# Three first loads on two queues: ScalarE's pair waits for a write of zeros, and two row blocks change queues

## The chip, the cores and the metric

The kernel runs on one core of a Trainium2 chip. The metric is the device time of one execution in microseconds (us). Before the change three runs took 220.27, 220.36 and 220.91 us, so the median is 220.36 us.

A core has five engines that run their own instruction lists and wait for each other by semaphores: TensorE (PE in the profile, its weight loads PEld), VectorE (DVE), ScalarE (ACT), GpSimd (POOL) and SyncE (SP). SP, ACT and POOL can also issue DMA transfers; all transfers are carried by the core's 16 DMA engines.

## What is computed

The input x has 2048 rows of 512 elements (bf16). Rows are normalised (mean and variance, no learned scale), and the result is the sum of x itself and of two branches over the normalised rows:

```python
xn = _layernorm(x)
# branch A: 32 heads of 16; features are softmax(+) and softmax(-) of q @ w_phi and k @ w_phi
kv  = einsum("bhsf,bhsd->bhfd", phi_k, v);  z = sum over s of phi_k
o   = (phi_q @ kv) / (phi_q @ z + 1e-6)
A   = o @ wo
# branch B: a gated product without a nonlinearity
B   = ((xn @ w_gate) * (xn @ w_up)) @ w_down        # 512 -> 1792 -> 512
out = x + A + B
```

q, k and v come from one matrix wqkv (512 x 1536); only its last third, wv, plays a part near the change.

## The kernel before, in words

The 2048 rows are cut into 16 blocks of 128 rows, x0 to x15, which lie in one tile `xall` (128 partitions x 16 blocks x 512). Four blocks make a group. Weights stay in SBUF: `wv` (the v third of wqkv, four chunks of 128 rows), `wg` and `wu` (gate and up), `wd` (down), `wo`, `wphi`, and `wT2`, which holds the k and q thirds of wqkv transposed.

The order on each engine is the order of the program text; nothing is rearranged by a scheduler. A tracker adds the semaphore waits that reads after writes, and writes after writes, need.

**The loads at the start** (lines 82 to 103). SP's queue issues x0, x2 and the second half of wv (chunks 2 and 3), then pieces of wg and wu, wphi, the transposed k third (wT2), x4 to x7, more of wg and wu, x8 to x15, wd and wo. ScalarE first loads its table and runs a one-column activation (`first`, line 90), and its queue issues x1 and the first half of wv (chunks 0 and 1). GpSimd's queue issues x3. Before its first real work VectorE fills small constants: `mhalf` (line 108) and the ones columns of five `vt` tiles (line 136).

**Warm-up.** TensorE has nothing to do until x arrives, so `warm_up` (line 309) gives it nine matmuls on a constant, seven of 512 columns and two of 128.

**The first four blocks** (lines 371 to 406). For a short way from the load to the first matmul these blocks are treated apart from the rest: instead of a full normalisation, `sub_sum` (line 338) writes D*x minus the row sum, and the row's scale is applied later.

- The row sums: block 0 by VectorE (`sum_of`, line 374), blocks 1 and 2 by ScalarE (line 378, an activation that also accumulates; the trace shows it as an ACTIVATE and a READ_ACCUMULATOR), block 3 by VectorE.
- `sub_sum` for all four on VectorE, block 0 in two halves.
- `lt` (line 206): four 128x128 transposes on TensorE per block, into one PSUM bank, and copies (line 207) into `xnT` by VectorE or ScalarE.
- `first_v` (line 237): x @ wv for a block, in two steps of two chunks; chunks 0 and 1 need the first half of wv, chunks 2 and 3 the second. The tiles are called kv for blocks 0 and 1 and pv for blocks 2 and 3.

VectorE's list at this place is: sum of x0, `sub_sum` of x0 (two halves), `sub_sum` of x1 (needs ScalarE's sum), two copies of block 0's transposes, `sub_sum` of x2, a copy of block 1, sum of x3, and so on. TensorE's list is: transposes of block 0, of block 1, `first_v(0)` chunks 0 and 1, transposes of block 2, `first_v(1)` and `first_v(2)` chunks 0 and 1, `first_v(0)` chunks 2 and 3, transposes of block 3, the rest of `first_v`, and then the long sequence of gate and up matmuls (`ffn`, lines 275 and 279), k and q features, attention and output (`fin`, lines 291 and 294), which fills the remaining time.

Of the kernel before, what the change touches and what calls it, by code (L numbers as in the profile page):

```python
# [21 lines left out]
def kernel(  # L22
# [12 lines left out]
    nc = tc.nc  # L35
    P = 128
    S, D = A_x.shape[-2], A_x.shape[-1]
# [19 lines left out]
    xall = xpool.tile([P, NT, D], BF16)  # L57
# [10 lines left out]
    def dma_x(lo, hi, eng=nc.sync):  # L68
        eng.dma_start(out=xall[:, lo:hi, :], in_=x_view[:, lo:hi, :])
# [4 lines left out]
    def dma_wv(lo, hi, eng):  # L74
        eng.dma_start(out=wv[:, lo:hi, :],
                      in_=A_wqkv[lo * P:hi * P, 2 * D:3 * D].rearrange("(c p) f -> p c f", p=P))
# [3 lines left out]
        dma_cols(nc.sync, wu, B_w_up, lo, hi)  # L80

    dma_x(0, 1)
    dma_x(2, 3)
    dma_wv(2, DC, nc.sync)

    ET = mybir.EngineType
# [1 line left out]
    ones = nc.const_aps.tensor(1.0, [P, P], BF16)  # L88
    first = consts.tile([P, 1], BF16)
    nc.scalar.activation(out=first[:], in_=ones[:, 0:1], func=AF.Exp, scale=1.0)  # L90
    dma_x(1, 2, nc.scalar)
    dma_wv(0, 2, nc.scalar)
    dma_x(3, 4, nc.gpsimd)
    dma_gu(0, 2 * P)
# [431 lines left out]
```

## Time and profile before

| | |
|---|---|
| median of three runs | 220.36 us |
| the profiled execution's own time | 220.46 us |
| its span (first to last instruction) | 218.8 us |
| TensorE matmul busy | 214.9 us, 98% of the span |
| VectorE, ScalarE, GpSimd busy | 64%, 41%, 34% of the span |
| granted TensorE clock | 1.00 in every stretch |
| TensorE's first warm-up matmul starts | 0.83 us |
| its first transpose starts | 4.34 us |
| its first matmul with wv starts | 5.20 us |

How to read it: the profile page has shares of busy time, a chain of work that ended last, and groups of instructions by line. The timeline lists instructions with their start and duration, both in us from the span's start; "x8" means eight instructions merged into one row, "[0.41 <-DVE xn L338]" that the engine had been idle for 0.41 us and what released it. A name such as ACTq or SPq is an engine's sequencer, which issues the DMAs. In the list of DMA issues the last number is the time from issue to landing. In the table of DMA queues q1 is SP's, q10 ScalarE's and q0 GpSimd's; the columns are packets, MB and the share of the 16 engines' time in the window asked for. A packet of x or of wv is one row of 512 bf16 elements, so a block of x is 128 packets. Matmuls are pipelined, so a TensorE row's duration overlaps the next one's, and the pace is read from start to start.

### The profile page before, as it was taken

Reading aid. Unit: us, or ns where it says so; the run is one execution under the profiler, and the core shown is the slowest. Engines: PE = TensorE matmul, PEld = TensorE weight load, DVE = VectorE, ACT = ScalarE, POOL = GpSimd, SP = SyncE. Lnnn points to the kernel's source line nnn. Section 1 sums busy time; section 2 is a strip of 40 time slices with the busy share of each in tenths; the row PEclk is TensorE's granted clock in tenths of the full one; section 3 lists DMA queues with packets and bytes.
Section 4 is the critical chain, followed back from the end, with each engine's and each line's share of the span. In section 5 each row is a group of like instructions: output and inputs, shape, how many; then the busy total and the mean of one; then the engine's idle time right before and its main releaser. Section 6 shows DMA issues by size and latency. Waiting matters only on the chain.

```text
span 218.8 us, 3493 instructions
## 1 busy us (share of the span) xinstructions
PE 214.9 (98%) x1291; PEld 103.1 (47%) x1291; DVE 141.0 (64%) x242; ACT 89.2 (41%) x159; POOL 74.9 (34%) x72
## 2 busy tenths in 40 slices
PE   8999999999999999999999999999999999999994
PEld 3444445454444444444544444444444444454443
DVE  4878867786598758576599773296655655454321
ACT  5545686569575875565435212141231322100000
POOL 4450843373357554636045333033123033000000
PEclk9999999999999999999999999999999999999999
DMA  5999996005202240202028355114461431412201
GB/s 198 286 297 372 372 219 136 2 0 51 48 0 49 51 94 2 48 3 48 1 43 105 76 114 114 37 24 96 96 70 30 95 72 28 96 48 72 69 30 48
DMA packets 48433, 19.91 MB, mean 91 GB/s; under 512 B 37504, under 2 KB 48384, under 8 KB 48416
## 3 DMA queue, kind: packets, MB, share of 16 engines
q1 hardware_dynamic: 47952, 19.16, 38.9%
q10 hardware_dynamic: 416, 0.39, 0.5%
q8 instruction: 10, 0.16, 0.3%
q0 software_dynamic: 48, 0.13, 0.2%
q14 instruction: 7, 0.06, 0.1%
HBM read 8.67 MB, written 2.10 MB: 49 GB/s over the span
## 4 chain that ended last, share of the span: by engine, by line
PE 97%; DMA 1%; DVE 1%; issue 0%
PE g L275 22%; PE fin L291 22%; PE u L279 22%; PE fin L294 6%; PE q L237 6%; PE k L237 6%; PE pv L237 6%; PE kv L331 2%; PE ab L465 2%; DMA xall<-in_A_x_dram 1%; PE kv L237 1%; PE tp L206 1%; PE pq L226 1%; DVE tot L374 0%; DVE xn L338 0%; DVE o_sb L301 0%
## 5 line engine op out<-in xcount | busy, mean ns | idle before, releaser
L275 PE MATMUL g<-xnT,wg 128*128 128x512 bf16 x224 | 57.5, 379 | 0.0
L279 PE MATMUL u<-xnT,wu 128*128 128x512 bf16 x224 | 57.5, 379 | 0.0
L254 POOL TENSOR_TENSOR phiq<-e,rsum 128x1024 bf16<-128x1024 f32 x16 | 30.9, 1933 | 63.5 <-DVE rsum L252 56.0
L283 DVE TENSOR_TENSOR hT<-u,g_sb 128x512 bf16<-128x512 f32 x56 | 37.0, 666 | 23.9 <-PE u L279 15.8
L282 ACT CAST g_sb<-g 128x512 bf16<-128x512 f32 x56 | 32.9, 587 | 46.8 <-PE g L275 46.5
L250 DVE TENSOR_REDUCE sums<-e 128x64 f32<-128x1024 f32 x32 | 38.9, 1216 | 20.1 <-ACT e L247 20.1
L291 PE MATMUL fin<-wd,hT 128*128 128x512 bf16 (+2 forms) x238 | 51.1, 366 | 0.0
L254 POOL TENSOR_TENSOR phik<-e,rsum 128x1024 bf16<-128x1024 f32 x16 | 30.9, 1932 | 39.6 <-DVE rsum L252 33.6
L279 PEld LDWEIGHTS <-wu 128*128 128x128 bf16 x224 | 21.9, 98 | 26.4
L291 PEld LDWEIGHTS <-hT 128*128 128x128 bf16 x238 | 22.4, 98 | 24.8
L275 PEld LDWEIGHTS <-wg 128*128 128x128 bf16 x224 | 21.1, 98 | 24.0
L237 PEld LDWEIGHTS <-xnT 128*128 128x128 bf16 x192 | 17.4, 98 | 18.2 <-ACT xnT L207 0.7
L301 DVE TENSOR_TENSOR o_sb<-fin,xall 128x512 bf16<-128x512 f32 (+2 forms) x13 | 8.5, 651 | 20.5 <-PE fin L294 20.5
L252 DVE RECIPROCAL rsum<-sums 128x64 f32<-128x64 f32 x32 | 17.7, 553 | 3.1
L294 PE MATMUL fin<-wo,oT 128*128 128x512 bf16 (+2 forms) x68 | 16.6, 366 | 0.0
L237 PE MATMUL k<-W1k,xnT 128*128 128x512 bf16 x64 | 16.4, 379 | 0.0
L237 PE MATMUL q<-W1q,xnT 128*128 128x512 bf16 x64 | 16.4, 378 | 0.0
L246 ACT ACTIVATE e<-q 128x512 f32<-128x512 f32 x12 | 7.2, 597 | 22.2 <-PE q L237 22.2
L237 PE MATMUL pv<-wv,xnT 128*128 128x512 bf16 x56 | 14.4, 379 | 0.0
L478 DVE TENSOR_TENSOR otok<-ab,rden 128x512 bf16<-128x512 f32 x16 | 11.1, 692 | 0.6
L323 ACT CAST vt<-pv 128x512 bf16<-128x512 f32 x12 | 7.0, 587 | 10.0 <-PE pv L237 10.0
L154 DVE BATCH_NORM_STATS2 stats<-xall 128x6 f32<-128x512 bf16 x16 | 10.6, 664 | 0.0
(63 smaller groups left out, 131.8 us busy)
## 6 DMA issues: line engine op xcount, KB each, us to landing
out_dram<-o_sb SPq DMA_DIRECT2D x15, 128.0 KB, 2.0
wd<-in_B_w_down_dram SPq DMA_DIRECT2D x1, 1792.0 KB, 15.8
xall<-in_A_x_dram SPq DMA_DIRECT2D x1, 1024.0 KB, 11.9
wg<-in_B_w_gate_dram SPq DMA_DIRECT2D x1, 640.0 KB, 7.7
wu<-in_B_w_up_dram SPq DMA_DIRECT2D x1, 640.0 KB, 10.4
xall<-in_A_x_dram SPq DMA_DIRECT2D x1, 512.0 KB, 4.5
wg<-in_B_w_gate_dram SPq DMA_DIRECT2D x1, 512.0 KB, 5.3
wu<-in_B_w_up_dram SPq DMA_DIRECT2D x1, 512.0 KB, 6.4
```

The source lines that it names most:

```text
L154: nc.vector.bn_stats(out=stats[:], in_=xall[:, n, :])
L237: nc.tensor.matmul(ps, lhsT=xnT[:, j, n * P:(n + 1) * P], rhs=w[:, j, :], start=(j == 0), stop=(j == DC - 1))
L250: nc.vector.tensor_reduce(out=sums[:], in_=ev, axis=AX.X, op=ALU.add)
L252: nc.vector.reciprocal(out=rsum[:].rearrange("p a b -> p (a b)"), in_=sums[:])
L254: nc.gpsimd.tensor_tensor(out=phi[:].rearrange("p g (x f) -> p (g x) f", f=DH), in0=ev, in1=rsum[:].to_broadcast((P, 2 * H, DH)), op=ALU.mult)
L275: nc.tensor.matmul(gps, lhsT=wg[:, c, f * P:(f + 1) * P], rhs=xnT[:, c, T * TT:(T + 1) * TT], start=(c == 0), stop=(c == DC - 1))
L279: nc.tensor.matmul(ups, lhsT=wu[:, c, f * P:(f + 1) * P], rhs=xnT[:, c, T * TT:(T + 1) * TT], start=(c == 0), stop=(c == DC - 1))
L282: nc.scalar.copy(out=g_sb[:], in_=gps)
L283: nc.vector.tensor_tensor(out=hTs[T][:, f, :], in0=ups, in1=g_sb[:], op=ALU.mult)
L291: nc.tensor.matmul(ps, lhsT=hTs[T][:, f, t4 * P:(t4 + 1) * P], rhs=wd[:, f, lo:lo + w], start=(f == 0), stop=False)
L294: nc.tensor.matmul(ps, lhsT=oTs[n][:, c, :], rhs=wo[:, c, lo:lo + w], start=False, stop=(c == DC - 1))
L478: nc.vector.tensor_tensor(out=o_tok[:].rearrange("p (b h d) -> p b h d", b=2, d=DH), in0=abv[:, :, :, 0:DH], in1=rden[:].to_broadcast((P, ...
```

## The change

SP's second load becomes x1 instead of x2, and ScalarE's first load becomes x2 instead of x1. In front of ScalarE's loads VectorE gets one new instruction, at the head of its list: it writes zeros over the first 256 columns of block 2 in `xall`. ScalarE's load of x2 writes the same bytes, so it must wait for that write, and the load of wv's first half stands behind it in the same list. The values are all overwritten by the load. In the built program the write is a memset of 128 words per partition, ScalarE's first load waits for a VectorE semaphore, and no other instruction of any engine is added or removed; ScalarE's first row sum (x1) now waits for SP's second load, its second (x2) for its own queue's first.

```diff
     dma_x(0, 1)
-    dma_x(2, 3)
+    dma_x(1, 2)
     dma_wv(2, DC, nc.sync)
...
     nc.scalar.activation(out=first[:], in_=ones[:, 0:1], func=AF.Exp, scale=1.0)
-    dma_x(1, 2, nc.scalar)
+    nc.vector.memset(xall[:, 2, 0:D // 2], 0.0)
+    dma_x(2, 3, nc.scalar)
     dma_wv(0, 2, nc.scalar)
     dma_x(3, 4, nc.gpsimd)
```

## The prediction

> **What bounds the kernel now.** I read the chain of work that ended last first, on the page and then in order of time for the first 16 us.
>
> ```profile
> PE 97%; DMA 1%; DVE 1%; issue 0%
> ```
>
> ```profile
> 0.79 2.45 DMA xall<-in_A_x_dram
> ...
> 3.27 0.70 DVE tot L374
> ...
> 3.99 0.30 DVE xn L338
> ...
> 4.34 1.07 PE tp L206 x8
> 5.40 0.54 PE kv L237 x2
> ...
> 9.50 0.86 PE g L275 x4
> ```
>
> From 4.34 us on the chain is TensorE to the end, and the table of stretches has TensorE busy in every us from 5.20 to 214. So a delay before TensorE's first wv matmul is passed on to the end, and a gain there is all that this change can bring; what I have to find is when that matmul (5.20) starts afterwards. The timeline of the first 8 us and the finer rows of VectorE and TensorE show what it waits for:
>
> ```profile
> 0.79 1.28 ACT L90 ACT_TABLE_LOAD   x1 [0.79 <-PEq L510]
> ...
> 0.85 0.40 ACTq L69 DMA_DIRECT2D xall<-in_A_x_dram  x1
> 0.86 0.06 DVE L108 MEMSET mhalf<- 128x4 f32 x1 [0.86 <-PEq L510]
> 1.00 0.62 DVE L136 MEMSET vt<- 128x32 bf16 x5
> ...
> 1.28 0.45 ACTq L75 DMA_DIRECT2D wv<-in_A_wqkv_dram  x1
> ...
> 3.57 0.63 ACT L378 ACTIVATE junk<-xall 128x512 bf16<-128x512 bf16 x1 [1.28 <-DMA xall<-in_A_x_dram]
> ...
> 4.11 0.19 ACT L378 ACTIVATION_READ_ACCUMULATOR junk<-xall 128x1 f32 x1
> ```
>
> ```profile
> 4.39 0.35 DVE L338 TENSOR_SCALAR xn<-xall,tot 128x512 bf16<-128x512 bf16 x1
> ```
>
> ```profile
> 4.77 0.29 DVE L207 COPY xnT<-tp 128x256 bf16<-128x256 bf16 x1
> ```
>
> ```profile
> 4.80 0.39 PE L206 MATMUL tp<-ident,xn 128*128 128x128 bf16 x2
> ```
>
> x1 lands at 0.85 + 2.7 = 3.55, ScalarE starts its sum at 3.57 and has it at 4.11 + 0.19 = 4.30, VectorE subtracts it at 4.39, TensorE transposes block 1 from 4.80. VectorE's list is in order, so the copy of block 0's transposes (4.77) also stands behind the subtraction for x1, although block 0 had been ready before. Block 0's way (x0 lands at 3.25, its sum, its two halves at 3.99 and 4.19) ends on VectorE at the same 4.39. x1's landing therefore has only about 0.05 us of slack: sum at 4.30, a handover of 0.05 (VectorE's first half ends at 4.28, TensorE's weight load starts at 4.33), subtraction at 4.39.
>
> **The change, part by part.**
>
> *The write of zeros.* A memset of 4 words takes 0.06 and one of 32 elements 0.09, so about 1.07 ns an element; 128 words give 0.06 + 124 x 1.07 ns = 0.19 us. Bounds: 0.09 (the 32-element row) and 0.33 (all 256 elements one by one). It starts where mhalf does, 0.86, and ends at 1.05. VectorE's other memsets move from their end at 1.62 to about 1.85; its next work is at 3.27, so this costs nothing.
>
> *ScalarE's wait.* With the handover of 0.05 its first load is issued at 1.10 instead of 0.85, 0.25 late (0.15 to 0.39), and wv's first half at 1.53 instead of 1.28. Behind the waiting instruction stand only that load and the sums of x1 and x2, which need x anyway. wv's first half lands at 1.53 + 3.4 = 4.93 (4.68 before), and TensorE wants it at 5.20 or later: covered by 0.27, and by more once TensorE is late itself. If that cover goes, see the second rival. x2 lands at 1.10 + 2.7 = 3.80, up to 4.0; its sum starts only behind that of x1, at 4.33 before: covered.
>
> *x1 in second place of SP's queue.* This is the price of the change. In the list of DMA issues ScalarE's first load (x1) and SP's second (x2) show the same 2.7 us to landing:
>
> ```profile
> xall<-in_A_x_dram ACTq DMA_DIRECT2D x1, 128.0 KB, 2.7
> xall<-in_A_x_dram SPq DMA_DIRECT2D x1, 128.0 KB, 2.7
> ```
>
> SP's second load is issued at 1.25, so x1 lands at 3.95 if nothing else changes: the upper bound, 0.40 later. The lower bound comes from the packets of the queues (q1 is SP's, q10 ScalarE's). By 2.5 us they had moved 71 and 19, by 3.0 us 168 and 110, and:
>
> ```profile
> q1 hardware_dynamic: 223, 0.21, 19.3%
> q10 hardware_dynamic: 155, 0.14, 13.2%
> ```
>
> by 3.25 us. q10's 128th packet moved at about 3.07 and x1 landed 0.48 later. If SP's queue had the DMA engines to itself, its 256th packet would have moved when both together had moved 256, at about 2.94, and x1 would land at 3.42, 0.13 sooner. Between the two: SP's 256th packet moved at about 3.39, when q10 was at some 177; with q10 0.25 late it would be at some 141, so 36 packets (36 KB, at the 352 GB/s of that stretch 0.10 us) go to SP, and x1 lands at 3.85. I take that value, since the row of the same place in the same queue is the nearest one and 0.25 us is a small part of the stretch in which the queues share: **x1 is 0.30 later**.
>
> *What follows.* Less the slack, the subtraction starts 0.25 later, at 4.64; the copies of block 0 and the transposes of block 1 follow it, and the first wv matmul starts at 5.45. A part comes back. Warm-up matmuls of 512 columns start 0.427 apart (weight loads at 2.49, 2.92, 3.35), those from 5.56 on 0.216 apart, and the one at 5.20 is 0.36 from its successor:
>
> ```profile
> 5.20 0.52 PE L237 MATMUL kv<-wv,xnT 128*128 128x512 bf16 x1
> ...
> 5.56 0.38 PE L237 MATMUL kv<-wv,xnT 128*128 128x512 bf16 x1
> ```
>
> So TensorE changes from half to full pace inside that matmul, after some 0.29 us of it, at 5.49, though the row of the granted clock reads 1.00 throughout. Started at 5.45 it takes 0.24 instead of 0.36. Sum: +0.25 - 0.12 = **+0.13 us**; when the pace changes earlier in a run, the whole +0.25. From 5.20 to 6.51 TensorE waited only 0.08 more, for ScalarE's copy of block 2, which moves with the rest. The other loads of SP's list keep their places; x4 to x7 (10.42) wait for ScalarE's first load, which is x2 now and lands over 6 us earlier.
>
> The profiled execution took 220.46, 1.66 more than its span and 0.10 above the median. 220.46 + 0.13 = 220.59 for it, 220.49 to 220.61 from the median with 0.13 to 0.25. I say 220.6. Its own range: bounds of x1's landing give -0.1 to +0.4, the three runs differ by 0.3%: 220.2 to 220.9. A difference under 0.3% (0.66 us) can't be told from none here.
>
> **Rivals.**
>
> 1. *x1 is not later at all*, as SP's queue has the engines nearly alone. Then x0 comes 0.12 sooner (both queues together had 128 packets at 2.60, SP's alone at 2.72) and x1 0.13, the wv matmul starts at 5.08, but runs at half pace until 5.49 (0.42 instead of 0.36): -0.12 + 0.06 = -0.06, 220.4. Against it: the write ends at 1.05, and the first packets move at about 1.8, so the loads are hardly "behind" x0. The Trainium skill, "DMA: Bandwidth & Descriptors", section "Queues, rings and completion order", says that an engine's completion mark lands only after all earlier writes of that engine, of all queues. That speaks for this rival: x0's last packet moved at 2.72 and it landed at 3.25, and without ScalarE's packets between, the 0.53 could shrink. Chance 0.06.
>
> 2. *Slower: ScalarE's queue waits for its engine too.* Before, its load left at 0.85, beside the table load (0.79 to 2.07). No row shows a load there that waits for a semaphore. If such a wait is only passed after what stands ahead of it is done (`first` ends at 2.29), x2 leaves at 2.30 and wv's first half at 2.73, landing at 6.13 instead of 4.68. The wv matmul then starts at 6.15 at full pace: its pair ends at 6.58 instead of 5.78, +0.8, 221.2. It decides as soon as wv's first half lands after about 5.4. For it: nothing but the missing row. Against it: the queue ran past the engine before. Chance 0.18.
>
> 3. *Slower: full pace comes later.* TensorE went to full pace 4.66 us after its first matmul (0.83 to 5.49), with a pause of 0.15 at 4.19 and one of 0.06 before 4.80. Now block 0's transposes are done at 4.74 and those of block 1 start at 5.05, a pause of 0.31. If a pause over the 0.15 that did no harm starts the count again at 5.05, full pace comes at 9.71, and 4.26 us of work go at half pace: +2.1, 222.6. Against it: the pause is short beside 4.66. The Trainium skill, "TensorE: Matmul & The Clock Gate", Part 1, gives the count as a busy window of about 3.4 us that runs freely, and Part 4 says that transposes do not count as busy; one window more would be, as an estimate, 1.7 us. The trace agrees with the half pace, but block 2's transposes at 5.78 start 0.055 apart, block 1's 0.107, so transposes do run at full pace. Chance 0.14.
>
> **Chances.** The forecast 0.46, rival 1 0.06: within 0.3%, 0.52. Rivals 2 and 3, and 0.06 for a landing later than any row here: slower, 0.38. For faster by 0.66 us x1 would have to land before 2.9, earlier than the packets can have moved; 0.10 for a cause that I do not see. The range takes in rival 2 and half of the faster side and leaves out rival 3 and the rest: 219.5 to 221.6.
>
> **What would show it.** ScalarE's first load should be issued at 1.0 to 1.24; at 2.3 rival 2 holds. ScalarE's first sum should start at 3.87 (3.44 in rival 1), VectorE's subtraction for block 1 at 4.64, TensorE's first wv matmul at 5.45 with the second 0.22 to 0.25 behind it; starts 0.43 apart far beyond 6 are rival 3. The forecast is wrong if the first wv matmul waits for wv, or if anything after 10 us differs by more than the shift.

## The result and the profile after

Thirteen runs of each kernel, taken in turns: 220.53 us before (220.27 to 220.95), 222.54 us after (221.04 to 225.27). The ratio is 1.008, with a 95% interval of 1.0056 to 1.0105; like the ratios of the experiments it leaves out runs more than 1.5% above the fastest of the same kernel (here three after, 224.51 and up), which is why it is below the 1.009 of the medians. So the change makes the kernel slower by about 1.8 us, and makes it scatter: before, all runs lie within 0.7 us, after, within 4.2.

The profiled execution took 222.06 us, 1.60 more than that of before, with a span of 220.4 instead of 218.8. Its chain of work, first the page's summary, then the first pieces in order of time (start, duration, what):

```profile
PE 96%; DMA 2%; ACT 0%; DVE 0%; issue 0%
```

```profile
0.79 0.74 ACT L90
1.52 0.03 issue
1.56 5.34 DMA wv<-in_A_wqkv_dram
6.90 0.04 issue
6.94 0.59 PE kv L238 x2
7.53 0.22 PE tp L207 x4
```

The chain no longer comes by way of x and its sum. It runs from ScalarE's issue of wv's first half (1.56) through one transfer of 5.34 us straight to TensorE's first wv matmul at 6.94, which was at 5.20. That is 1.74 later; the pair of matmuls then runs at full pace and takes 0.43 (block 2's transposes start at 7.37) instead of 0.58, and 1.74 - 0.15 = 1.59 is the whole difference of the two spans. The timeline of the first 9 us shows that everything ahead of that went much as before:

```profile
0.79 1.28 ACT L90 ACT_TABLE_LOAD   x1 [0.79 <-PEq L511]
...
0.89 0.17 DVE L91 MEMSET xall<- 128x128 uint32 x1 [0.89 <-PEq L511]
...
1.09 0.44 ACTq L69 DMA_DIRECT2D xall<-in_A_x_dram  x1
...
1.56 0.45 ACTq L75 DMA_DIRECT2D wv<-in_A_wqkv_dram  x1
...
1.71 0.43 SPq L75 DMA_DIRECT2D wv<-in_A_wqkv_dram  x1
...
3.84 0.63 ACT L379 ACTIVATE junk<-xall 128x512 bf16<-128x512 bf16 x1 [1.55 <-DMA xall<-in_A_x_dram]
...
4.60 0.35 DVE L339 TENSOR_SCALAR xn<-xall,tot 128x512 bf16<-128x512 bf16 x1 [0.33 <-ACT junk L379]
...
5.01 0.47 PE L207 MATMUL tp<-ident,xn 128*128 128x128 bf16 x4 [0.27 <-DVE xn L339]
...
6.94 0.59 PE L238 MATMUL kv<-wv,xnT 128*128 128x512 bf16 x2 [1.46 <-DMA wv<-in_A_wqkv_dram]
```

Block 1 is transposed at 5.01 (4.80 before), and then TensorE waits 1.46 us for wv. The load was issued 0.28 later than before, but took 5.34 us to land instead of 3.4. How far the queues were at 4.5 us (packets, MB, share of the engines' time; q1 SP, q10 ScalarE), before and then after:

```profile
q1 hardware_dynamic: 306, 0.28, 18.7%
q10 hardware_dynamic: 416, 0.39, 25.5%
```

```profile
q1 hardware_dynamic: 318, 0.29, 19.5%
q10 hardware_dynamic: 251, 0.24, 19.2%
```

All of ScalarE's 416 packets (384 rows of 1 KB, which are the 0.39 MB, and 32 small ones) had moved before the change, 251 after it; SP's queue had hardly gained. In the stretch from 3.5 to 3.75 us the engines as a whole were slow. The last two columns are their busy share and GB/s, before and then after:

```profile
3.50:3.75 0.25, 0.25 (x2) 0.00 (x0) 0.25 (x1) 0.18 (x1) 0.20 (x1) 1.00 1.07 377
```

```profile
3.50:3.75 0.25, 0.25 (x2) 0.00 (x0) 0.25 (x1) 0.00 (x0) 0.20 (x1) 1.00 0.50 135
```

The fall from 377 to 135 GB/s says that this is more than a fair sharing of full engines.

### The profile page after: what moved, and what is told of

It is laid out like the page before. It is cut to its first block, busy times and chain, and to the rows that moved or that the text cites. A ratio compares the mean times of both kernels' runs of the same rounds, so it can differ in the third digit from the quotient of the medians.

```text
span 220.4 us, 3494 instructions
## 1 busy us (share of the span) xinstructions
PE 214.9 (98%) x1291; PEld 103.0 (47%) x1291; DVE 141.3 (64%) x243; ACT 89.2 (40%) x159; POOL 75.0 (34%) x72
## 4 chain that ended last, share of the span: by engine, by line
PE 96%; DMA 2%; ACT 0%; DVE 0%; issue 0%
PE g L276 22%; PE fin L292 22%; PE u L280 22%; PE fin L295 6%; PE k L238 6%; PE q L238 6%; PE pv L238 6%; DMA wv<-in_A_wqkv_dram 2%; PE kv L332 2%; PE ab L466 2%; PE kv L238 1%; PE pq L227 1%; ACT L90 0%; PE tp L207 0%; DVE o_sb L302 0%
```

## The experiments

All times of issue, landing and first wv matmul are from each kernel's one profiled execution, in us; "third" is the issue of the load that SP's queue has in third place (its second half of wv, unless said otherwise). Medians of the experiments are of 4 to 10 runs (e13 has one). The ratio is against 13 to 31 runs of the kernel before in the same turns, whose medians were 220.48 to 220.86. A row's landing and its median need not belong together: the profiled executions of e3, e5 and e8 are among the faster of theirs (221.01, 221.17 and 221.25), that of e1 is the slowest.

| kernel | wv first half issued | SP's third | took | landed | first wv matmul | median | ratio, interval |
|---|---|---|---|---|---|---|---|
| before | 1.28 | 1.71 | 3.4 | 4.7 | 5.20 | 220.53 | 1 |
| after | 1.56 | 1.71 | 5.3 | 6.9 | 6.94 | 222.54 | 1.0080 (1.0056 to 1.0105) |
| e1 exchange alone | 1.28 | 1.72 | 4.0 | 5.3 | 6.02 | 220.72 | 1.0020 (1.0001 to 1.0039) |
| e2 write alone | 1.54 | 1.71 | 5.3 | 6.8 | 6.87 | 222.00 | 1.0081 (1.0034 to 1.0127) |
| e3 wv ahead of x2 | 0.85 | 1.72 | 3.0 | 3.9 | 5.67 | 221.79 | 1.0062 (1.0033 to 1.0092) |
| e4 SP's half later | 1.56 | 1.72 (wg) | 4.9 | 6.5 | 6.48 | 222.61 | 1.0100 (1.0072 to 1.0128) |
| e5 x3 by SP | 1.54 | 1.71 | 4.5 | 6.0 | 6.06 | 222.23 | 1.0047 (1.0019 to 1.0075) |
| e6 before, x3 by SP | 1.27 | 1.71 | 3.4 | 4.7 | 5.19 | 220.75 | 1.0002 (0.9989 to 1.0015) |
| e7 short write | 1.38 | 1.72 | 3.6 | 5.0 | 5.44 | 221.03 | 1.0029 (0.9997 to 1.0061) |
| e8 long write | 1.66 | 1.72 | 4.4 | 6.1 | 6.13 | 222.43 | 1.0076 (1.0049 to 1.0103) |
| e9 SP's third waits too | 1.55 | 2.15 | 3.9 | 5.5 | 5.52 | 220.78 | 1.0023 (0.9998 to 1.0047) |
| e10 before, SP's half second | 1.28 | 1.72 (x2) | 4.2 | 5.5 | 5.57 | 222.81 | 1.0101 (1.0062 to 1.0140) |
| e11 before, SP's third waits | 1.27 | 2.02 | 3.4 | 4.7 | 5.17 | 220.55 | 1.0002 (0.9990 to 1.0014) |
| e12 SP's third waits less | 1.54 | 1.89 | 5.5 | 7.0 | 7.05 | 222.15 | 1.0067 (1.0036 to 1.0098) |
| e13 nothing else to move | 1.53 | 3.32 | 3.3 | 4.8 | 5.09 | 221.25 (1 run) | |
| e14 before, only wv waits | 1.62 | 1.72 | 5.7 | 7.3 | 7.36 | 223.88 | 1.0127 (1.0066 to 1.0188) |
| e15 both halves wait | 1.62 | 2.69 | 4.2 | 5.8 | 5.90 | 221.11 | 1.0029 (0.9995 to 1.0063) |

### Which part of the change: e1 and e2

e1 leaves the write out, e2 keeps the loads as before and adds the write in front of ScalarE's x1.

```diff
 # e1, against the changed kernel
-    nc.vector.memset(xall[:, 2, 0:D // 2], 0.0)
 # e2, against the kernel before
+    nc.vector.memset(xall[:, 1, 0:D // 2], 0.0)
     dma_x(1, 2, nc.scalar)
```

> The exchange alone: SP loads x0, x1, ScalarE x2, and the write of zeros is left out, so ScalarE's queue issues at 0.85 and 1.28 as before. Theory L (the loss is the late issue of wv's first half: with its lead over SP's half of wv, issued at 1.71, cut from 0.43 to 0.15 us, the DMA engines serve both halves side by side): the first half lands near 4.7 and the first wv matmul starts at 5.3 to 5.5, later than 5.20 only by x1's later landing; time 220.4 to 220.9. Theory X (the exchange does it, x1's landing and what follows it in SP's queue): the first wv matmul starts near 6.9 and the time is near 222.5.

> The write alone: the loads as before (SP x0, x2, ScalarE x1), with the write of zeros over x1's first 256 columns, so that ScalarE's queue issues x1 at 1.09 and wv's first half at 1.56. Theory L: wv's first half lands near 6.9, the first wv matmul starts near 6.9, time near 222.5, with the wide scatter of the changed kernel. Theory X: 5.2 to 5.4 and 220.4 to 220.8.

e2 alone gives the whole loss: wv's first half lands at 6.8, the first wv matmul starts at 6.87, the ratio is 1.0081. Its timeline has the same wait:

```profile
6.87 0.59 PE L238 MATMUL kv<-wv,xnT 128*128 128x512 bf16 x2 [1.42 <-DMA wv<-in_A_wqkv_dram]
```

e1 costs 0.2% (220.72, against 220.48 before in the same turns). Its one profiled execution is not a typical run (222.45, the slowest of ten): x0, issued at 0.79 as in the other kernels, was summed from 3.85 instead of 3.27, x1 landed at 4.4, wv's half at 5.3 instead of the forecast 4.7, and TensorE stayed at half pace until 8.9, of which more below. Theory X, that the exchange does it, fell.

### Is it the lateness of wv's half: e3, e7, e8

```diff
 # e3, against the changed kernel
+    dma_wv(0, 2, nc.scalar)
     nc.vector.memset(xall[:, 2, 0:D // 2], 0.0)
     dma_x(2, 3, nc.scalar)
-    dma_wv(0, 2, nc.scalar)
 # e7
-    nc.vector.memset(xall[:, 2, 0:D // 2], 0.0)
+    nc.vector.memset(xall[:, 2, 0:2], 0.0)
 # e8
-    nc.vector.memset(xall[:, 2, 0:D // 2], 0.0)
+    nc.vector.memset(xall[:, 2, :], 0.0)
```

> The change, but ScalarE's queue issues wv's first half before the load that waits for the write: wv's half at 0.85, x2 behind it at about 1.3. Theory L: wv's half keeps its lead over SP's half (0.86 us), lands by 4.7, the first wv matmul starts at 5.3 to 5.6 and the time is 220.4 to 221.0. A theory W, that any load on ScalarE's queue behind a semaphore makes the queue slow, would put x2's landing near 5 or later, and the time at 221 or more. Theory X: near 222.5.

> The change with a write of two columns instead of 256, so that ScalarE's queue issues at about 0.99 and 1.45, half way between the two kernels. If the loss grows step by step with the lateness of the issue, wv's first half lands at 5.3 to 6.3, the first wv matmul starts there, and the time is 220.9 to 221.7. If it is a threshold (in front of GpSimd's packets or not), it is like the exchange alone (220.7) or like the change (222.5).

> The change with a write of all 512 columns, some 0.13 us longer: ScalarE's queue issues at about 1.22 and 1.69, nearly beside SP's half of wv (1.71). Step by step: wv's first half lands at 7.0 to 7.6 and the time is 222.7 to 223.5. Threshold: like the change, 222 to 222.8.

In e3 wv's half is there at 3.9 and TensorE never waits for it; the first wv matmul starts at 5.67, just past the forecast's 5.6, because now x1 (4.25) and x2 (5.0) land late. This execution took 221.01, so that delay is cheap. The median of 221.79 was outside what I had written for theory L, but no run lies near it: five took 220.93 to 221.11 and five 222.48 to 223.12. No run of the slower five was profiled, and what made them slow is open. Theory W, that a load behind a semaphore makes ScalarE's queue slow, has both of its signs here (x2 at 5 or later, 221 or more). Against it stand x2 of the changed kernel, which waits for the same write and took 2.4 us, and e13 below, where it took 2.2 and wv's half behind it 3.3.

In e7, issued at 1.38, the half lands at 5.0, no later than x1's way allows, and the time is between the two kernels, not told from either the exchange alone or a small loss (seven runs up to 221.24, three from 222.08 to 223.33). In e8, issued at 1.66, it landed at 6.1 in the profiled execution, where a growth step by step had 7.0 to 7.6, and the median is that of the changed kernel. So the loss does not grow step by step: beside SP's third load at 1.71 the half took 3.6 us when issued at 1.38, and 4.4 to 5.7 when issued at 1.54 to 1.66.

### What slows it: e4, e5, e6

```diff
 # e4, against the changed kernel: SP's half of wv behind the first pieces of wg and wu
-    dma_wv(2, DC, nc.sync)
...
     dma_gu(0, 2 * P)
+    dma_wv(2, DC, nc.sync)
 # e5 against the changed kernel, e6 against the kernel before
-    dma_x(3, 4, nc.gpsimd)
+    dma_x(3, 4)
```

> The change, but SP's half of wv is issued behind the first pieces of wg and wu, at about 2.7 instead of 1.71. Theory L in its form 'side by side with the other half of wv': with that half away, wv's first half lands near 4.7 and the first wv matmul starts near 5.4; the second half comes late and the step that needs it waits, so the time says little. Theory L in the form 'whatever SP's queue has next takes the engines': wg's piece is issued at 1.71 in its place, and the first wv matmul starts at 6 or later again.

> The change, but x3 is loaded by SP behind its half of wv, not by GpSimd, so that no transfer of GpSimd's queue is under way. Theory G (the slow stretch begins when GpSimd's packets do: in the changed kernel wv's first half moves 13 to 36 packets in each quarter us from 3.5 to 5.25, beside GpSimd's 48, and 89 in each before the change, when it was ahead of them): wv's first half lands by 5.2, the first wv matmul starts at 5.4 to 5.6 and the time is 220.4 to 221.2. Theory R (SP's queue alone shares the engines with ScalarE's, packet for packet): it lands at 6.5 to 6.9 as before, 221.5 to 222.5.

> Control: the kernel before, with x3 loaded by SP behind its half of wv instead of by GpSimd. Both theories: the first wv matmul starts at 5.2 as before, wv's second half and x3 may come some tenths of a us later, 220.2 to 221.0. If x3's own place costs something, it shows here.

e4: with wg's piece in third place of SP's queue instead of wv's other half, wv's first half still lands at 6.5. So it is not the two halves as such; the second form of theory L held. (Its median of 222.61 has the late second half in it, which lands at 8.85.) e5: without any transfer of GpSimd the half lands at 6.0 in the profiled execution, between theory G (by 5.2) and theory R (6.5 to 6.9), and the time is not better than the change's by more than the intervals allow (222.23). Theory G fell as the whole cause; GpSimd's packets take at most a part. The control e6 is the kernel before, within 0.15%.

### Lead or lateness: e9 to e12

In e9 SP's half of wv waits as well, for a second VectorE write (ones over that half, which its load overwrites), so that SP's queue goes on at 2.15 instead of 1.71. e12 has a shorter second write, e11 has only that second write, in the kernel before. e10 is the kernel before with SP's loads exchanged, no write.

```diff
 # e9, against the changed kernel; e12 with [:, 2:DC, 0:384]; e11 in the kernel before
-    dma_wv(2, DC, nc.sync)
...
     dma_x(3, 4, nc.gpsimd)
+    nc.vector.memset(wv[:, 2:DC, :], 1.0)
+    dma_wv(2, DC, nc.sync)
 # e10, against the kernel before
-    dma_x(2, 3)
     dma_wv(2, DC, nc.sync)
+    dma_x(2, 3)
```

> The change, and SP's half of wv waits too, for a second VectorE write (1.0 over that half, about 1.1 us, all overwritten by the load), so that SP's third load and all behind it are issued at about 2.2 instead of 1.71, 0.65 after ScalarE's load of wv's first half (1.56). In every trace so far the engines' busy share falls for a quarter us or more between 3.25 and 4.5 (0.50 in the changed kernel at 3.5), and wv's first half has come wholly before that dip or behind it. Theory H1 (what counts is the lead over SP's third load): the first half lands by 5.1 and the first wv matmul starts at 5.4 to 5.6, though the second half is late (7 or more), so the time is 221 to 222.5. Theory H2 (what counts is the issue itself: a load issued later than about 1.4, when the first packets are about to move, gets its packets moving only behind the dip): the first half lands at 6 or later and the first wv matmul starts there.

> The kernel before, without any write, with SP's list x0, second half of wv, x2: SP's half of wv is issued at about 1.25, beside ScalarE's first half (1.28), and x2 at about 1.7. H1: the two halves of wv are side by side, so the first half lands at 6 or later and the first wv matmul starts at 6.2 or later, 221.5 or more. H2: both halves come before the dip and land at 4.7 to 5.3, x2, issued at 1.7, lands behind it at 5 or later instead of 3.95, so that the first wv matmul starts at 5.2 to 5.5 and what waits is the subtraction for block 2; time 220.6 to 221.5.

> The kernel before, with no write over x, but SP's half of wv waits for the VectorE write of 1.0 over it (about 0.9 us), so that SP's third load is issued at about 2.0 instead of 1.71 and ScalarE's wv half leads it by 0.7 instead of 0.43. If a lead of 0.43 was already enough, x1 and wv's first half land as before (3.5, 4.7), the first wv matmul starts at 5.1 to 5.2 and the time is 220.3 to 220.9. If a longer lead still helps, x1 lands 0.1 sooner and the time can be 220.1 to 220.4, below the kernel before.

> The change with the second write cut to 384 of 512 columns, so that SP's third load is issued at about 1.95 and the lead of ScalarE's wv half over it is 0.4 instead of 0.15 in the change and 0.6 in the run with the whole second write. Theory H1 (the lead counts, and from 0.34 up it is enough): wv's first half lands by 5.5, the first wv matmul starts at 5.4 to 5.7, time 220.6 to 221.1. If instead SP's third load has to be issued after about 2.1, when the engines are busy with x: first wv matmul at 6 or later, 221.5 or more.

e9 is the change with its loss taken away by moving what comes after it. ScalarE's load is issued at 1.55 as in the changed kernel, but it lands at 5.5, and the timeline has

```profile
5.52 0.59 PE L239 MATMUL kv<-wv,xnT 128*128 128x512 bf16 x2
```

without a wait. H1 had the half by 5.1 and 221 to 222.5, so it landed later than that and the time is better; 220.78 lies in the 220.2 to 220.9 that the prediction had worked out for the change. e12, with SP's queue going on at 1.89, has the whole loss again (7.05 in its profiled execution, a median of 222.15). So H1 in my form, that a lead of 0.34 is enough, fell, and H2, that the issue time alone decides, fell with e9. e10 fits neither wholly: with SP's half in second place the first half took 4.2 and landed at 5.5 (H1 had said 6 or later, H2 5.3 at most), and x2, now third in SP's queue and issued at 1.72, took 4.5 us to 6.2 and made the time 222.81. Whether that is the same loss on another tile, or only x2's place in SP's queue behind 256 KB that landed at 5.3, is not shown. e11: where nothing is late, moving SP's third load away brings nothing that can be measured (1.0002), so no version here beats the kernel before.

### Competition or lateness: e13, e14, e15

```diff
 # e13, against the changed kernel: SP's third load and all behind it, x3 too, after a GpSimd write
-    dma_wv(2, DC, nc.sync)
-    dma_x(3, 4, nc.gpsimd)
...
     _block_rows(nc.gpsimd, BO[:], 8, DH, E1)
+    nc.gpsimd.memset(wv[:, 2:DC, :], 1.0)
+    dma_wv(2, DC, nc.sync)
+    dma_x(3, 4)
...
 # e14, against the kernel before (e15: and the second write of e9)
     dma_x(1, 2, nc.scalar)
+    nc.vector.memset(wv[:, 0:2, 0:320], 1.0)
     dma_wv(0, 2, nc.scalar)
```

> The change, but SP issues its half of wv, x3 (instead of GpSimd) and all that follows only after a GpSimd write over that half of wv, at about 3.5 to 4, so that behind x0, x1 and x2 only wv's first half is there to be moved. If others' packets slow it (competition), it moves 80 to 90 packets in each quarter us from 3.25 on, lands by 4.9 and the first wv matmul starts at 5.4 to 5.6. If its own lateness does it (H2), it moves under 40 in the quarters after 3.5 and lands at 5.5 or later. The time itself says nothing here, as the second half of wv and x3 come late; about 223 to 225.

> The kernel before, where only ScalarE's load of wv's first half waits for a VectorE write (over part of its own bytes), so that it is issued at about 1.55 while x0, x1 and x2 are issued as before. If its issue time alone decides, the first half lands at 6 or later, the first wv matmul starts there and the time is 221.5 to 223. If x's loads have to be late too, it lands by 5.2, and the time is 220.4 to 221.0.

> As the run before this one, and SP's half of wv waits for a second VectorE write as well, so that it is issued at about 2.5. Competition: the first half lands by 5.2 to 5.5 and the time is 220.5 to 221.2, as in the run where the change had both writes. H2: it lands at 6 or later and the time is 221.5 or more.

e13 is a single run, and in it the half, issued at 1.53, as late as in the changed kernel, took 3.3 us. It moved 67 to 70 packets in each quarter us from 3.25 to 4.0 (competition had 80 to 90, H2 under 40 from 3.5). At 4.5 us its queues stand as those of the kernel before, not as those of the changed one:

```profile
q1 hardware_dynamic: 304, 0.28, 20.6%
q10 hardware_dynamic: 415, 0.39, 27.9%
```

and the first wv matmul starts at 5.09, with x1 summed from 3.69 (3.84 in the changed kernel):

```profile
3.69 0.63 ACT L379 ACTIVATE junk<-xall 128x512 bf16<-128x512 bf16 x1 [1.41 <-DMA xall<-in_A_x_dram]
```

(The time of that run, 221.25, has the late x3 in it; I had expected 223 to 225. As x3 is held back too, e13 takes away GpSimd's transfer as well as SP's; e5 had taken away GpSimd's alone, and the half took 4.5.) e14 is the other side: with x0, x1 and x2 issued as before and only wv's half late, beside SP's unchanged list, the half took 5.7 us. e15 moves SP's third load to 2.69 and the half takes 4.2. It lands at 5.8, between competition (5.2 to 5.5) and H2 (6 or later); the time, 221.11, is at the upper end of what competition had been given, where H2 had 221.5 or more.

Shown, then: the loss comes of the late issue of wv's first half together with what SP's queue issues right behind it. The write brings it without the exchange (e2), and with ScalarE's issue just as late it is gone, in nine of ten runs, when SP's third load and all behind it leave some 0.4 us later (e9: 220.78). In the six kernels where the half was issued at 1.54 to 1.66 and SP's third load 0.06 to 0.35 later (after, e2, e5, e8, e12, e14), and in e4 with wg in that place, it took 4.4 to 5.7, in all others 3.0 to 4.2. These are single executions, and only 0.2 lies between the two groups (4.2 in e10 and e15, 4.4 in e8), so they do not say how sharp the boundary is.

What stays open is how the loads hinder each other, and why 1.54 with 1.89 (e12) loses and 1.55 with 2.15 (e9) does not. It is not that SP's packets take the turns. In e12 SP's queue moved none from 3.5 to 4.5 us, standing at 288, its third load issued at 1.89, and ScalarE's moved only 85, from 177 (221 before the change). At 4.5 us:

```profile
q10 hardware_dynamic: 262, 0.25, 20.9%
q1 hardware_dynamic: 288, 0.26, 17.7%
```

GpSimd's queue moved 24 in that time, and the engines as a whole had a busy share of 0.60 and moved 157 GB/s (1.05 and 354 before the change).

### The scatter

e14 also shows a second cost, which some of the slow runs seem to share. Its page has a fall in the row of the granted clock, its mean clock is 0.992, and its timeline, in three stretches, shows what that is:

```profile
PEclk9799999999999999999999999999999999999999
```

```profile
7.36 0.59 PE L238 MATMUL kv<-wv,xnT 128*128 128x512 bf16 x2 [2.22 <-DMA wv<-in_A_wqkv_dram]
```

```profile
8.62 1.06 PE L238 MATMUL pv<-wv,xnT 128*128 128x512 bf16 x2
```

```profile
10.76 1.05 PE L238 MATMUL kv<-wv,xnT 128*128 128x512 bf16 x2
11.61 1.49 PE L238 MATMUL pv<-wv,xnT 128*128 128x512 bf16 x6
```

TensorE stood still for 2.22 us, started at 7.36 at full pace, fell back to half pace at about 8.3 (matmuls of 512 columns 0.43 apart) and was at full pace again at about 11.6 (six matmuls in 1.33). So 3.3 us at half pace, 1.7 us lost on top. The Trainium skill, "TensorE: Matmul & The Clock Gate", Part 1, says that a window of about 3.4 us of idling puts the clock back to half and a busy one lifts it; the trace agrees with the length of the slow stretch, though here the pause was 2.2 us. Without the transposes in between, TensorE paused from the end of the warm-up at 4.19 to 7.36, 3.17 us; in e12 that pause was 2.86 us, to 7.05, and the pace did not fall. Which of the two lengths counts is not shown. Three of the changed kernel's thirteen runs have the same mean clock of 0.992 (223.98, 224.07, 224.51), and three of e14's four (223.70 to 224.79). That these runs of the changed kernel had such a pause is inferred from the clock; their traces were not taken. Its two slowest, 225.10 and 225.27, have a mean clock of 1.0, and what made them slow is open. So is what parts the runs of e3 and of e7 into two groups, all with a mean clock of 1.0; e1's profiled execution shows that late first loads and a late change to full pace together can put a run 1.7 us above the median with a mean clock of 0.999.

## Why the prediction was wrong

The predicted 220.6 (219.5 to 221.6) missed 222.54, and the chance of slower was put at 0.38.

- **The step that failed** is "wv's first half lands at 1.53 + 3.4 = 4.93 ..., covered by 0.27". I took the 3.4 us of before as a property of the load and moved it by the 0.25 of the issue. It landed at 6.90. The first wv matmul waited for wv, the sign that the prediction had named against itself. In its place the runs show that the time to landing hangs on when the other queue's next loads are issued: with the half issued at 1.53 to 1.56 it was 5.3 in the changed kernel, 3.9 in e9 with SP's third load 0.44 later, and 3.3 in e13 with it at 3.32. By what mechanism is open.
- The packets that I read for x1's landing also showed it: before, SP's queue stood at 288 packets (256 rows, its two blocks of x, and 32 small ones) from 3.75 to 4.25 while ScalarE's moved 131, so wv's first half had the engines nearly to itself. (That alone does not make it fast, as e12 shows.) I had noticed that the queues share, and worked it out for x1 alone, not for the load behind it on the moved queue.
- *The write, the wait and x1* were right: write 0.17 (predicted 0.19), ScalarE's issue at 1.09 and 1.56 (1.10 and 1.53), first sum at 3.84 (3.87), subtraction at 4.60 (4.64), transposes of block 1 at 5.01 (5.05). Those alone are the +0.13 to +0.25; e9, which has all of them, measured 220.78 and a ratio of 1.0023 (0.9998 to 1.0047). The 3.85 for x1's landing came out better than its working: a queue's packets hold 16 small ones for each of these loads (416 are 384 rows and 32), so the 128th and the 256th are not the last of a block, and SP's queue reached its 256th about 0.05 sooner, not 0.10. That it was so near is in part luck.
- *Rival 1* had a part: x0 was summed from 3.07 instead of 3.27, and block 0 transposed from 4.13, but block 1 held the chain as predicted.
- *Rival 2* had the right place, the right point from which it decides (wv's half landing after 5.4) and, with +0.8, half the price; its mechanism was wrong. ScalarE's queue did not wait for its engine: 1.09 lies inside the table load (0.79 to 2.07).
- *Rival 3* did not happen in the profiled execution (full pace at 6.94), but something like it did elsewhere: in e14 after a pause of 2.22, and in e1's profiled execution, where full pace came at about 8.9. Whether e1's longer pause (4.19 to 4.91) decided that is open, since the change of pace also lay at 5.49 in the kernel before and at about 6.2 in e6, whose first wv matmuls are timed alike.

## What to carry to other kernels

A transfer's time to landing, read from one trace, belongs to that order of issues; when a load is moved in time, list what the other queues will have issued by then, and bound its landing by the slowest load near that place in the trace (here SP's half of wv: 4.4 us, issued at 1.71), not by its own old row. That would have given 5.9, past the 5.4 from which it decides, though still short of the 6.9 measured. Price the cover of every load behind the moved one, not only of the one that the change names. Where several queues start together, the load with the least cover belongs in the earliest issue slot (here x1; with wv's half there instead, e3 had a median of 221.79), and holding back the loads that nobody waits for yet can be worth as much as issuing the needed one sooner (e9 against the change: 220.78 against 222.54).

## What was not expected of the hardware

- 0.28 us of later issue became 2.2 us of later landing (4.7 to 6.9, with 3.4 and 5.3 us from issue to landing), and from 3.5 to 3.75 the engines moved 135 GB/s at a busy share of 0.50 where they had moved 377 before.
- The Trainium skill, "DMA: Bandwidth & Descriptors", section "Issuing engines are not separate DMA queues", says that loads of different issuers interleave on the same 16 engines and that several issuers only save issue time. The runs agree that the queues are not independent, but not that only issue time is at stake: e12 and e13 issue wv's half at the same time and it lands at 7.0 and 4.8.
- In e14 TensorE started at full pace after its 2.22 us pause and fell back to half pace 0.9 us later, and the page's row of the granted clock showed that fall, but not the half pace at the start of every run.
